# Attention and feed-forward on one core: where the maxima units of the next pair stand between the score tiles

## The chip, the cores and the metric

The kernel runs on 1 core of one Trainium2 chip. The metric is the device time of one execution in microseconds, as the median of several executions. The core has TensorE (PE: matmuls, and its weight loads, PEld), VectorE (DVE), ScalarE (ACT), GpSimd (POOL), and SyncE (SP), which issues most DMAs. Each has its own instruction stream, in order, and they wait for each other by semaphores. TensorE writes to PSUM, from where VectorE and ScalarE read.

## The reference

The inputs are q, k and v of 8 batches, 8 heads, 1152 positions and 64 features, and the weights w_in (512 x 2048) and w_out (2048 x 512).

```python
q_pool = q.reshape(B, H, S // factor, factor, D).mean(axis=3)          # 576 queries
scores = scale * np.matmul(q_pool, k.transpose(0, 1, 3, 2))            # 576 x 1152
scores = scores - np.max(scores, axis=-1, keepdims=True)
attn = np.exp(scores)
attn = attn / (np.sum(attn, axis=-1, keepdims=True) + 1e-09)
attn_out = np.matmul(attn, v)
x = attn_out.transpose(0, 2, 1, 3).reshape(B * S, H * D)               # 4608 x 512
h = x @ w_in
out = (h - np.tanh(h)) @ w_out
```

All of it is in fp32. Since the maximum of a query's scores is subtracted before the exponential, it has to be known (to some digits) before the scores of that query are used.

## The kernel before

There are two stages. The attention stage goes over 32 *pairs* (a pair is two heads of one batch; the two heads lie on the two halves of the 128 partitions). The feed-forward stage then goes over 9 chunks of 512 tokens. The change lies in the attention stage.

**A pair.** Its main loop (L475 to L491) has a score stage and a value stage of 18 *places* each. A place is one of 9 tiles of 128 keys for one of two halves of the queries, 288 of 576; so place 9 is key tile 0 of the second half, and a place of the score stage is called a tile below. At each place of the score stage `scores` (L278) issues eight matmuls of 288 columns into one PSUM tile: four terms, each for both heads. The terms are high part of the keys times high part of the queries (`kq_h` alone in the profile), high times low and low times high (`kq_l,kq_h` and `kq_h,kq_l`), and minus the maximum (`m_row,sel`). ScalarE then takes the exponential into a tile `p`, and POOL adds up three `p` tiles at a time (`add_p`, L295). In the value stage each place has two matmuls of `p` and `v` for each query half's output. Then `sums` adds the partial sums by matmuls with ones.

**The maxima.** The maxima of a pair are computed one pair ahead, by 14 *units*. A unit (`max_part`, L240) issues two matmuls of 384 columns, one for each head, from high parts alone, into one PSUM tile, and VectorE reduces it to maxima (`TENSOR_REDUCE mx<-ps 128x2`). Twelve units (0 to 11: four blocks of 128 queries by three thirds of the keys) are put behind places of the score stage of the pair before. Two more (12 and 13, for the last 64 queries of both heads, through `q_last`) stand behind the sums of the pair before that; unit 13 has one matmul and a narrow reduce (`128x1`). `max_row` (L258), at the last score place, turns the maxima into a row by a transpose and two DMAs through DRAM.

**The ring.** Score tiles, units, the two outputs of the value stage and the sums share one ring of four PSUM tiles of two banks each (L164), which are given out in turn in the order of the program. So each of them can be written only when the one four before it has been read: a score tile by ScalarE's exponential, a unit by VectorE's reduce.

**What sets the order.** Every engine's instructions stay in the order in which the program issues them (`InOrder`, L27). A table `at` lists functions to be called behind each place (`add`, L404; `run`, L470): the units (L407 to L413), the loads and splitting of later pairs (L414 to L425), and the first chunk of the feed-forward stage (L432 to L437), for which in the last pairs `x_r` is fetched from DRAM, and VectorE multiplies (place 8), ScalarE rounds (place 9) and VectorE subtracts (place 12). In the value stage four pieces of work on the weights go to VectorE and ScalarE.

Of the kernel before, what the change touches and what calls it, by code (L numbers as in the profile page):

```python
# [46 lines left out]
def attention_ffn_kernel(  # L47
# [107 lines left out]
    with ExitStack() as actx:  # L155
# [248 lines left out]
        def add(pi, place, f, *args):  # L404
            at.setdefault((pi, place), []).append(lambda: f(*args))

        for pi in range(1, n_pair):  # L407
            for i in range(12):
                add(pi - 1, i // 2 * 3 + 1 + i % 2, max_part, pi, i)
            if pi >= 2:  # L410
                for i in range(12, 14):
                    add(pi - 2, 2 * NS, max_part, pi, i)
            add(pi - 1, NS - 1, max_row, pi)  # L413
# [247 lines left out]
```

## Time and profile before

| | us |
|---|---|
| median of 3 runs | 1612.94 (1612.37 to 1613.27) |
| the profiled execution's own time | 1613.26 |
| its span, first to last instruction | 1611.5 |
| TensorE busy | 1578.1 (98%) |
| VectorE busy | 1207.5 (75%) |
| GpSimd busy | 1116.1 (69%) |
| ScalarE busy | 988.3 (61%) |
| mean granted TensorE clock | 0.996 |

All helpers issue through one line, L37, so the profile is read by engine and tile name: `ps<-kq_h` with 288 columns is a score matmul, with 384 columns one of a unit; `mx<-ps` is a unit's reduce, `p<-ps` an exponential. A row of a timeline has start, length, engine, line, operation, tiles, shape and count, and in brackets the idle time before it and what ended that. Alike instructions that follow each other are merged (x2, x4), from the first's start to the last's end. A TensorE instruction's length runs to its modelled end, so that matmuls overlap; what they occupy is the distance between starts. Where TensorE had to wait, the first matmul after the wait is listed from its weight load on, and the second one's start, less one matmul, gives the time from which it counts.

### The profile page before, as it was taken

What the parts mean: (1) busy time and instruction counts of PE and PEld (TensorE: products, weight loads), DVE (VectorE), ACT (ScalarE), POOL (GpSimd) and SP (SyncE); (2) the same over time, 40 slices, a digit from 0 to 9 for tenths busy, and PEclk for the clock granted to TensorE, in tenths of its full rate; (3) what the DMA queues carried; (4) which work ended last, traced back from release to release, by engine and by line L of the source; (5) the groups of instructions that cost most, each with busy time, mean ns of one, the idle gap of its engine ahead of it and who ended that gap; (6) DMA issues with size and microseconds to landing.
All of it is one profiled execution on the core that took longest, in us unless ns stands there. A gap on an engine that the chain in (4) does not pass through costs nothing.

```text
span 1611.5 us, 30812 instructions
## 1 busy us (share of the span) xinstructions
PE 1578.1 (98%) x12012; PEld 1224.9 (76%) x12012; DVE 1207.5 (75%) x1590; ACT 988.3 (61%) x1615; POOL 1116.1 (69%) x780
## 2 busy tenths in 40 slices
PE   5999999999999999998999999999999999999998
PEld 4777677777777777776678888888888888888886
DVE  6588788897878888766267777777777777777776
ACT  4676677676676677665455655565555555565554
POOL 3787787787787787786647566666657576666654
PEclk9999999999999999999999999999999999999999
DMA  5547767758577767637180201011010102020000
GB/s 174 170 145 209 224 197 228 215 173 281 160 241 209 232 195 222 178 115 221 62 329 14 66 13 66 7 42 38 7 66 14 66 14 66 13 67 14 27 1 27
DMA packets 84068, 193.59 MB, mean 120 GB/s; under 512 B 12370, under 2 KB 38994, under 8 KB 81874
## 3 DMA queue, kind: packets, MB, share of 16 engines
q1 hardware_dynamic: 79458, 164.20, 29.1%
q0 software_dynamic: 4464, 27.43, 8.7%
q8 instruction: 94, 1.54, 0.4%
q14 instruction: 52, 0.43, 0.1%
HBM read 126.12 MB, written 38.04 MB: 102 GB/s over the span
## 4 chain that ended last, share of the span: by engine, by line
PE 95%; DVE 2%; DMA 2%; ACT 1%; issue 0%; SPq 0%; POOLq 0%; POOL 0%; ACTq 0%; DVEq 0%
PE ps L37 46%; PE ps_h L37 25%; PE ps_o L37 24%; DMA x_r<-r_dram 1%; DVE mx L37 1%; DMA q<-in_q_dram 0%; DMA w_raw<-wi_dram 0%; DVE ps_w L37 0%; ACT g_s L37 0%; ACT kq_h L37 0%; ACT p L37 0%; DVE kq_l L37 0%; DVE x_r L37 0%; DMA m_dram<-tr 0%; SPq L37 0%
## 5 line engine op out<-in xcount | busy, mean ns | idle before, releaser
L37 DVE TENSOR_REDUCE mx<-ps 128x2 f32<-128x768 f32 x448 | 395.4, 924 | 117.3 <-PE ps L37 117.3
L37 ACT ACTIVATE p<-ps 128x576 f32<-128x576 f32 x576 | 353.1, 653 | 86.8 <-PE ps L37 62.7
L37 POOL TENSOR_TENSOR sum<-p,p 128x576 f32<-128x576 f32 x192 | 281.9, 1468 | 146.6 <-ACT p L37 146.6
L37 POOL TENSOR_SCALAR g_m<-g_u 128x512 uint8<-128x512 f32 (+1 forms) x145 | 246.9, 1703 | 195.7 <-ACT g_u L37 180.6
L37 POOL TENSOR_TENSOR sum<-sum,p 128x576 f32<-128x576 f32 x192 | 298.7, 1556 | 15.1
L37 PE MATMUL ps<-kq_h 64*128 64x288 f32 (+1 forms) x1920 | 286.1, 343 | 16.1 <-ACT kq_h L37 7.7
L37 PE MATMUL ps<-p,v 128*64 128x288 f32 x2304 | 286.4, 407 | 0.0
L37 POOL TENSOR_TENSOR g_lo<-g_s,g_hi 128x512 fp32r<-128x512 f32 (+1 forms) x145 | 186.6, 1287 | 93.7 <-ACT g_hi L37 93.7
L37 PEld LDWEIGHTS ps<-p,v 128*64 128x64 f32 x2304 | 162.6, 137 | 114.2 <-ACT p L37 6.6
L37 PE MATMUL ps_o<-w,g_hi 128*128 128x512 f32 x792 | 244.6, 390 | 1.0 <-ACT g_hi L37 1.0
L37 DVE SCALAR_TENSOR_TENSOR ps_w<-g_u,ps_h 128x512 f32<-128x512 f32 (+1 forms) x145 | 100.4, 692 | 187.6 <-ACT g_t L37 187.5
L37 ACT ACTIVATE g_u<-ps_h 128x512 f32<-128x512 f32 (+1 forms) x145 | 85.8, 592 | 241.9 <-PE ps_h L37 240.2
L37 PEld LDWEIGHTS ps<-kq_h 64*128 64x128 f32 x1920 | 181.9, 187 | 64.7 <-ACT p L37 27.5
L37 PE MATMUL ps_h<-x_h,w 128*128 128x512 f32 (+1 forms) x800 | 214.8, 390 | 0.0
L37 ACT ACTIVATE g_s<-g_u,pc 128x512 f32<-128x512 f32 x290 | 193.2, 714 | 11.9 <-ACT g_u L37 0.4
L37 PEld LDWEIGHTS ps_h<-x_h,w 128*128 128x128 f32 x800 | 149.7, 188 | 32.4
L37 PEld LDWEIGHTS ps_o<-w,g_hi 128*128 128x128 f32 x792 | 148.5, 188 | 33.6 <-ACT g_hi L37 1.4
L37 PE MATMUL ps<-kq_l,kq_h 64*128 64x288 f32 x1152 | 171.0, 293 | 0.0
L37 PE MATMUL ps<-kq_h,kq_l 64*128 64x288 f32 x1152 | 170.9, 293 | 0.0
L37 PE MATMUL ps<-m_row,sel 64*128 64x288 f32 x1152 | 170.8, 293 | 0.0
L37 PE MATMUL ps_o<-w,g_lo 128*128 128x512 f32 x396 | 154.8, 391 | 0.6 <-POOL g_lo L37 0.5
L37 DVE COPY_PREDICATED g_s<-g_m,g_t 128x512 f32<-128x512 uint8 (+1 forms) x145 | 111.0, 765 | 17.8 <-DVE g_t L37 3.7
(94 smaller groups left out, 2365.4 us busy)
## 6 DMA issues: line engine op xcount, KB each, us to landing
kq_l<-raw POOLq DMA_DIRECT2D x31, 864.0 KB, 10.7
raw<-in_k_dram SPq DMA_DIRECT2D x32, 576.0 KB
q<-in_q_dram SPq DMA_DIRECT2D x32, 576.0 KB
v<-in_v_dram SPq DMA_DIRECT2D x32, 576.0 KB
x_dram<-o_s SPq DMA_DIRECT2D x32, 288.0 KB
x_l<-x_dram SPq DMA_DIRECT2D x9, 1024.0 KB
out_dram<-o_f SPq DMA_DIRECT2D x36, 256.0 KB
w_raw<-in_w_in_dram SPq DMA_DIRECT2D x8, 1024.0 KB
```

The lines of the kernel that those rows point to most:

```text
L37: i = f(*args, **kwargs)
```

## The change

The twelve units of the next pair are called behind other places. Before, two stood behind each three key tiles: behind 1, 2, 4, 5, 7, 8, 10, 11, 13, 14, 16 and 17. Now they stand behind 0, 2, 3, 4, 5, 6, 8, 9, 11, 13, 15 and 17.

```diff
         for pi in range(1, n_pair):
             for i in range(12):
-                add(pi - 1, i // 2 * 3 + 1 + i % 2, max_part, pi, i)
+                add(pi - 1, (0, 2, 3, 4, 5, 6, 8, 9, 11, 13, 15, 17)[i], max_part, pi, i)
             if pi >= 2:
                 for i in range(12, 14):
                     add(pi - 2, 2 * NS, max_part, pi, i)
             add(pi - 1, NS - 1, max_row, pi)
```

On TensorE, the start of a pair (here pair 1; units 12 and 13 read `q_last`, `ps_594` is tile 0, 384 columns are a unit) stood so before, with the first matmul of each tile or unit and the engine that it waits for:

```order
L37 MATMUL ps_587<-kq_h_521,q_last0_122 128x384 [waits DVE_49,Activation_49]
...
L37 MATMUL ps_591<-kq_h_521,q_last0_122 128x384 [waits Activation_49]
L37 MATMUL ps_594<-kq_h_221 128x288 [waits Activation_49]
...
L37 MATMUL ps_605<-kq_h_221 128x288 [waits Activation_49]
...
L37 MATMUL ps_618<-kq_h_521 128x384 [waits DVE_49]
...
L37 MATMUL ps_622<-kq_h_221 128x288 [waits DVE_49]
...
L37 MATMUL ps_634<-kq_h_521 128x384 [waits Activation_49]
...
L37 MATMUL ps_640<-kq_h_221 128x288 [waits Activation_49]
```

and now:

```order
L37 MATMUL ps_594<-kq_h_221 128x288 [waits Activation_49]
...
L37 MATMUL ps_605<-kq_h_521 128x384 [waits Activation_49]
...
L37 MATMUL ps_609<-kq_h_221 128x288 [waits DVE_49]
...
L37 MATMUL ps_622<-kq_h_221 128x288 [waits DVE_49]
...
L37 MATMUL ps_634<-kq_h_521 128x384 [waits Activation_49]
...
L37 MATMUL ps_640<-kq_h_221 128x288 [waits DVE_49]
...
L37 MATMUL ps_651<-kq_h_521 128x384 [waits Activation_49]
...
L37 MATMUL ps_655<-kq_h_221 128x288 [waits Activation_49]
```

Unit 0 (`ps_605` now, `ps_618` before) has moved ahead of tile 1. Tile 1 (`ps_609`) has unit 12 four places before it and waits for VectorE, where tile 1 before (`ps_605`) had the sums and waited for ScalarE. Tile 3 (`ps_640`) now waits for unit 0's reduce.

On VectorE the units keep their order; only in the last pairs do they move past the operations on `x_r` and `x_l` of the first feed-forward chunk:

```order
-L37 TENSOR_REDUCE mx<-ps 128x2 x6
+L37 TENSOR_REDUCE mx<-ps 128x2 x7
 L37 TENSOR_TENSOR x_r<-x_l,x_r 128x512
 L37 TENSOR_REDUCE mx<-ps 128x2 x2
 L37 TENSOR_TENSOR x_l<-x_r,x_h 128x512
-L37 TENSOR_REDUCE mx<-ps 128x2 x4
+L37 TENSOR_REDUCE mx<-ps 128x2 x3
```

Seven of the twelve units, where there were six, stand ahead of the multiplication by `x_r`, and three, where there were four, behind the subtraction.

## The prediction

> **What bounds the kernel now.** I read the page first. TensorE fills the span, and nearly the whole chain of waits that ended last is its own.
>
> ```profile
> PE 1578.1 (98%) x12012; PEld 1224.9 (76%) x12012; DVE 1207.5 (75%) x1590; ACT 988.3 (61%) x1615; POOL 1116.1 (69%) x780
> PE 95%; DVE 2%; DMA 2%; ACT 1%; issue 0%; SPq 0%; POOLq 0%; POOL 0%; ACTq 0%; DVEq 0%
> ```
>
> That busy figure hides short waits, so I went to the stages: for one pair the score stage, the value stage, and the sums with the last two maxima units; then the score stage of the last pair but one, and of the last pair, which has no units in it.
>
> ```profile
> core 0: us, PE busy (x) PEld busy (x) DVE busy (x) ACT busy (x) POOL busy (x), PEclk, DMA share, GB/s
> 390.25:403.06 12.81, 12.81 (x169) 11.43 (x169) 11.00 (x13) 10.42 (x17) 10.42 (x8) 1.00 0.86 283
> 403.06:411.94 8.88, 8.88 (x74) 5.08 (x73) 7.54 (x9) 5.92 (x7) 8.72 (x6) 1.00 0.34 103
> 411.94:414.35 2.41, 2.41 (x31) 1.25 (x29) 1.61 (x4) 0.82 (x2) 0.21 (x1) 1.00 1.05 288
> 753.43:774.74 21.31, 15.40 (x168) 14.18 (x169) 13.23 (x15) 11.14 (x18) 14.54 (x11) 0.84 0.60 179
> 785.32:794.94 9.62, 9.62 (x144) 9.45 (x145) 0.00 (x0) 9.25 (x18) 7.33 (x6) 1.00 0.10 37
> ```
>
> A score stage without units takes 9.62 us; twelve units add 3.19, or 0.266 each. TensorE needs less for one. A score matmul of 288 columns follows the last after 0.13 us (the first four rows below), so a unit of 384 columns needs 0.13 x 384/288 = 0.175. Twelve are 2.1, so about 1.1 us of each score stage is waiting. The timelines of TensorE, its weight loads, VectorE and ScalarE show where, in the pair that starts at 414.25:
>
> ```profile
> 417.02 0.30 PE L37 MATMUL ps<-kq_h 64*128 64x288 f32 x2
> 417.15 0.30 PE L37 MATMUL ps<-kq_l,kq_h 64*128 64x288 f32 x2
> 417.28 0.30 PE L37 MATMUL ps<-kq_h,kq_l 64*128 64x288 f32 x2
> 417.41 0.30 PE L37 MATMUL ps<-m_row,sel 64*128 64x288 f32 x2
> ...
> 414.48 0.30 PE L37 MATMUL ps<-kq_l,kq_h 64*128 64x288 f32 x2
> 415.41 0.65 PE L37 MATMUL ps<-kq_h 64*128 64x384 f32 x4
> 415.89 0.29 PE L37 MATMUL ps<-kq_l,kq_h 64*128 64x288 f32 x2
> ...
> 426.90 0.34 PE L37 MATMUL ps<-kq_h 64*128 64x384 f32 x2
> 427.17 1.19 PE L37 MATMUL ps<-p,v 128*64 128x288 f32 x8
> ```
> ```profile
> 415.65 0.19 PEld L37 LDWEIGHTS ps<-kq_h 64*128 64x128 f32 x2 [0.19 <-DVE mx L37]
> 418.53 0.19 PEld L37 LDWEIGHTS ps<-kq_h 64*128 64x128 f32 x2 [0.15 <-ACT p L37]
> ```
> ```profile
> 414.18 1.42 DVE L37 TENSOR_REDUCE mx<-ps 128x2 f32<-128x768 f32 x2 [0.73 <-PE ps L37]
> 415.79 1.84 DVE L37 TENSOR_REDUCE mx<-ps 128x2 f32<-128x768 f32 x2 [0.19 <-PE ps L37]
> 417.93 1.82 DVE L37 TENSOR_REDUCE mx<-ps 128x2 f32<-128x768 f32 x2 [0.30 <-PE ps L37]
> 420.07 1.82 DVE L37 TENSOR_REDUCE mx<-ps 128x2 f32<-128x768 f32 x2 [0.33 <-PE ps L37]
> 415.15 1.19 ACT L37 ACTIVATE p<-ps 128x576 f32<-128x576 f32 x2 [1.07 <-PE ps L37]
> L37 DVE TENSOR_REDUCE mx<-ps 128x2 f32<-128x768 f32 x248 | 227.2, 953 | 61.3 <-PE ps L37 61.3
> L37 DVE TENSOR_REDUCE mx<-ps 128x1 f32<-128x384 f32 x19 | 10.4, 547 | 0.0
> L37 ACT ACTIVATE p<-ps 128x576 f32<-128x576 f32 x342 | 210.3, 650 | 50.6 <-PE ps L37 35.9 <-POOL sum L37 5.2
> ```
>
> A score tile or unit can be written only when the one four places ahead of it in the ring of four PSUM tiles has been read. Before the change three key tiles with two units repeat every 2.14 us (VectorE's rows at 417.93 and 420.07), against 3 x 0.53 + 2 x 0.175 = 1.94 of work. The 0.2 goes mostly on the tile behind the second unit, which waits for an exponential (idle 0.15 at 418.53). Neither ScalarE (two exponentials in 1.19, one 0.65: one each 0.54, 1.62 of 2.14) nor VectorE (idle 0.3 per three tiles) is full: it is the round trip through four tiles that binds.
>
> **The change part by part.** Nothing is added or removed: 31 x 12 units and their reduces keep their number, size and order among themselves, and the DMA queues of SP and POOL keep theirs. What moves is which tile stands four ahead. I cost the new order by the longest path through a pair, from five steps read off these rows (the trace has a third digit where the rows have two, and I use it). Time 0 is the first score matmul, 414.48 - 0.13 = 414.35.
> (a) A key tile is 0.53, a unit 0.175 on TensorE.
> (b) From a unit's matmul to its reduce: 415.41 to 415.79, 0.372.
> (c) A reduce lasts 0.954; two without idle time take 1.82 to 1.84, so the second starts 0.876 after the first.
> (d) From a reduce's end to TensorE at work again: 414.18 + 1.42 = 415.60 to 415.89 - 0.13 = 415.76, so 0.157.
> (e) From a tile's first matmul to its exponential 0.79, and 0.65 for that; from its end also 0.157.
>
> Run on the old order, these steps put the last unit at 12.54; the rows have 426.90 - 414.35 = 12.55. So the steps can be trusted to about 0.01 in an order that they know.
>
> New order. Unit 0 goes out at 0.53, directly behind tile 0. Tile 1 now has the wide unit 12 four places ahead, whose reduce ends at 414.18 + 0.954 = 415.13, or 0.79; so tile 1 starts at 0.95 where it could at 0.70: a wait of 0.24. (Before, the tile behind unit 0 waited 0.17 for the narrow unit's reduce, the row at 415.65.) Tile 2 follows at 1.48, the unit behind it at 2.01, its reduce at 2.38. From here VectorE has five units in a row, one behind each of tiles 2 to 6, and TensorE offers one every 0.7 us where a reduce takes 0.876: the reduces run without idle time, the fifth from 2.38 + 4 x 0.876 = 5.88 to 6.84. Tile 9 stands four places behind that unit, so it starts at 6.84 + 0.157 = 7.00. The unit behind it is reduced from 7.00 + 0.53 + 0.372 = 7.90 to 8.86; tile 12 waits for that until 9.02; two tiles on, the unit behind 13 goes out at 10.08 and is reduced by 11.41; tile 16 starts at 11.57, and the last unit at 12.63.
>
> So the sum for an ordinary pair is +0.09 (12.63 for 12.54). The rarer, shorter waits of tiles 10 to 17 (0.02 and 0.06 per two tiles) save about 0.4 us, and the first half gives more than that back: with seven units behind nine tiles VectorE sets its pace. The exponentials have slack all along this path.
>
> The value stage starts 0.27 behind the last unit in both orders (426.90 to 427.17), so the 0.09 passes on. The last reduce ends about 0.1 earlier against it, which helps VectorE's weight work and costs nothing. POOL starts its additions 0.4 later, since the second exponential moves from 1.34 to 1.7; its cover is this:
>
> ```profile
> 409.06 2.28 POOL L37 TENSOR_TENSOR sum<-sum,p 128x576 f32<-128x576 f32 x1
> 411.94 1.66 PE L37 MATMUL ps<-sum,ones 128*32 128x288 f32 x24
> ```
>
> Its last addition ends at 411.34, 0.6 ahead of the first sums matmul; 0.6 - 0.4 + 0.09 is left. Without that cover the price would be up to 0.3 a pair.
>
> The last pair but one is special: VectorE and, behind it, ScalarE wait for x_r from DRAM, and TensorE stands still until 767.92.
>
> ```profile
> 765.98 0.69 DVE L37 TENSOR_TENSOR x_r<-x_l,x_r 128x512 f32<-128x512 f32 x1 [5.00 <-DMA x_r<-r_dram]
> 766.58 1.81 DVE L37 TENSOR_REDUCE mx<-ps 128x2 f32<-128x768 f32 x2
> 767.24 1.17 ACT L37 ACTIVATE p<-ps 128x576 f32<-128x576 f32 x2
> 767.92 0.61 PE L37 MATMUL ps<-kq_h 64*128 64x288 f32 x2 [5.91 <-ACT p L37]
> 768.33 0.44 PE L37 MATMUL ps<-kq_l,kq_h 64*128 64x288 f32 x2
> 768.57 0.44 PE L37 MATMUL ps<-kq_h,kq_l 64*128 64x288 f32 x2
> ```
>
> The landing does not move. Tile 12 waited for an exponential that ended at 767.24 + 0.65; now it waits for the reduce that starts at 766.58 and ends at 767.54, 0.3 sooner. And one unit fewer is left: three instead of four, at the slow pace of 0.24 per matmul (768.33 to 768.57; the clock of that stage is 0.84) 0.32 each. Together -0.5, where a later landing would leave -0.3. In the pair before that, where VectorE has two more operations, the same steps give +0.08. The first pair I leave at 0: its first tiles run at the slow pace, where the reduces of units 12 and 13 are done in time.
>
> Sum: 29 x 0.09 - 0.5 = +2.1 us on the profiled execution's 1613.26 us, 1615.4. That execution lies 0.3 above the median of the runs, 1612.94, so the median should be 1615.0, 0.13% up.
>
> Bounds. A run of five reduces does not occur in the trace; runs of two do. At worst each would take its full 0.954: the path gains 4 x 0.08 = 0.31 and the old order loses a little too, +0.32 a pair. At best only the elements count: wide less narrow reduce is (953 - 547)/384 = 1.06 ns per element, 0.81 for 768, and other waits then bind: -0.03 a pair. I take 0.876, which is measured on this instruction back to back, and 0.86 to 0.89 as its doubt: +0.04 to +0.13 a pair.
> [...]
>
> **The rivals.**
> *Slower: the reduces of a run do not overlap.* Place: tiles 2 to 9 of each pair. From 0.90 per reduce on it costs 0.16 a pair or more; at 0.954, 29 x 0.32 - 0.5 = +8.8, 1621.7. For it: no run of five is on record, and POOL adds at the same time. Against: every run of two in the rows quoted takes 1.82 to 1.84 with POOL adding throughout. Chance 0.18.
> *Faster: VectorE comes to the pair earlier.* If unit 12's reduce ends before 0.54, tile 1 no longer waits, and with all of VectorE's work 0.4 sooner the path ends at 12.39: -0.15 a pair, 29 x -0.15 - 0.5 = -4.9, 1608.0. For it: VectorE idles 0.73 before that reduce (row at 414.18). Against: it idles for TensorE's own matmuls of unit 12, and nothing ahead of tile 0 moves. Chance 0.09.
> *No change: waits are traded one for one.* The old order loses 1.06 a pair in waits and the new 1.15 by my steps; an error of 0.02 in two or three steps makes them equal. Then only the -0.5 stays, and the few tenths of the first and last pairs: 1611.5 to 1614. Chance 0.20.
> The change does reach TensorE's queue as written, so that it does nothing at all is left out.
>
> **How the numbers follow.** The forecast has 0.53: 1615.0, alone 1614.0 to 1616.3. What a measurement of this kernel can tell from no change is 0.2%, 3.2 us, that is 1609.7 to 1616.2. Within it lie nearly all of the forecast and the traded waits, 0.69; above it, the non-overlapping reduces and the forecast's edge, 0.21; below it, most of the earlier VectorE and little else, 0.10. The range 1611.0 to 1618.5 takes in the forecast, the traded waits and the milder third of the slower case.
>
> **What would show it.** In the changed kernel's ordinary pairs the score stage should last 12.9 (12.81 now). Behind unit 0 a weight load should wait some 0.2 to 0.3 for a VectorE reduce. VectorE's row should merge five or more reduces in 4 x 0.876 + 0.954 = 4.46 us with no idle time, and the tile behind unit 8 should wait 0.17 for it. ScalarE's releases should no longer be the main ones in the weight loads' waits. The value stage should keep 8.88 and the sums 2.41. I am wrong if five reduces take over 4.6 us, if tile 1 starts by 0.75, or if a pair differs by more than 0.15.

## The result, and the profile after

The changed kernel takes 1616.49 us (median of 12 runs, 1612.64 to 1617.45) beside 1612.32 of the kernel before in the same comparison (12 runs, 1610.70 to 1614.11): a ratio of 1.0022, with 95% between 1.0013 and 1.0031. A second comparison on another occasion gave 1614.49 (11 runs) beside 1612.80 (27 runs), 1.0014 [1.0005, 1.0022]. So it is slower by 0.05 to 0.3%, on the edge of the 0.2% that can be told from no change; the forecast was 1615.0, 0.13% up.

The profiled execution took 1615.31 us, with a span of 1613.5 (1611.5 before). On the page, busy times and the chain's shares by engine are almost those of before; VectorE is busy for 11 us more (1218.6 for 1207.5) and has 3% of the chain instead of 2%:

```profile
PE 1580.7 (98%) x12012; PEld 1226.9 (76%) x12012; DVE 1218.6 (76%) x1590; ACT 991.1 (61%) x1615; POOL 1117.4 (69%) x780
PE 94%; DVE 3%; DMA 2%; ACT 1%; issue 0%; SPq 0%; POOLq 0%; POOL 0%; DVEq 0%; ACTq 0%
```

The stages of one pair (score, value, sums with the last two units), then the score stages of the last pair but one and of the last pair:

```profile
core 0: us, PE busy (x) PEld busy (x) DVE busy (x) ACT busy (x) POOL busy (x), PEclk, DMA share, GB/s
391.27:404.15 12.88, 12.88 (x168) 11.48 (x168) 11.24 (x13) 10.49 (x17) 10.10 (x8) 1.00 0.88 281
404.15:413.03 8.88, 8.88 (x74) 5.08 (x72) 7.42 (x8) 5.93 (x8) 8.72 (x6) 1.00 0.30 90
413.03:415.46 2.43, 2.43 (x31) 1.26 (x30) 1.95 (x4) 0.82 (x2) 0.55 (x1) 1.00 1.13 294
756.42:775.72 19.30, 14.54 (x168) 13.02 (x169) 13.34 (x15) 11.23 (x18) 13.37 (x10) 0.91 0.66 207
786.30:795.92 9.62, 9.62 (x144) 9.46 (x144) 0.00 (x0) 9.24 (x18) 7.32 (x6) 1.00 0.09 35
```

The score stage has grown from 12.81 to 12.88; value stage, sums and the stage without units are as they were (8.88, 2.43 here and 2.41 or 2.42 elsewhere, 9.62). The score stage of the last pair but one (the row at 756.42) is 2.0 shorter than before (21.31), which comes up below.

Inside the score stage, the pair that starts at 415.46. First VectorE's reduces, then two weight loads that waited, then TensorE, and last POOL's additions of the pair before and of this one around the sums' matmuls:

```profile
415.29 2.29 DVE L37 TENSOR_REDUCE mx<-ps 128x2 f32<-128x768 f32 x3 [0.41 <-PE ps L37]
417.84 4.42 DVE L37 TENSOR_REDUCE mx<-ps 128x2 f32<-128x768 f32 x5 [0.27 <-PE ps L37]
422.45 1.84 DVE L37 TENSOR_REDUCE mx<-ps 128x2 f32<-128x768 f32 x2 [0.20 <-PE ps L37]
...
416.29 0.19 PEld L37 LDWEIGHTS ps<-kq_h 64*128 64x128 f32 x2 [0.25 <-DVE mx L37]
422.31 0.19 PEld L37 LDWEIGHTS ps<-kq_h 64*128 64x128 f32 x2 [0.17 <-DVE mx L37]
...
415.59 0.29 PE L37 MATMUL ps<-kq_l,kq_h 64*128 64x288 f32 x2
...
416.54 0.29 PE L37 MATMUL ps<-kq_l,kq_h 64*128 64x288 f32 x2
...
422.54 0.29 PE L37 MATMUL ps<-kq_l,kq_h 64*128 64x288 f32 x2
...
428.08 0.34 PE L37 MATMUL ps<-kq_h 64*128 64x384 f32 x2
428.35 0.95 PE L37 MATMUL ps<-p,v 128*64 128x288 f32 x6
...
410.48 2.28 POOL L37 TENSOR_TENSOR sum<-sum,p 128x576 f32<-128x576 f32 x1
413.03 1.18 PE L37 MATMUL ps<-sum,ones 128*32 128x288 f32 x16
417.93 1.42 POOL L37 TENSOR_TENSOR sum<-p,p 128x576 f32<-128x576 f32 x1 [4.35 <-ACT p L37]
```

Five reduces run without idle time from 417.84 on, in 4.42. Two weight loads of the score stage wait for VectorE, by 0.25 (tile 1, behind unit 0) and by 0.17 (tile 9, behind the unit that follows tile 8, which the prediction calls unit 8). The value stage still starts 0.27 behind the last unit (428.08 to 428.35). POOL begins its additions 2.47 after the pair's start, where it was 2.07, and ended those of the pair before at 412.76, 0.27 ahead of the sums.

Over the pairs in the middle of the program the group of the score matmuls' weight loads shows who is waited for. Before:

```profile
L37 PEld LDWEIGHTS ps<-kq_h 64*128 64x128 f32 x1142 | 106.8, 183 | 27.4 <-ACT p L37 12.6 <-ACT s_s L37 4.9 <-DVE mx L37 3.6
```

and after, over the same pairs:

```profile
L37 PEld LDWEIGHTS ps<-kq_h 64*128 64x128 f32 x1142 | 106.7, 183 | 28.5 <-DVE mx L37 8.7 <-ACT s_s L37 5.0 <-ACT p L37 0.3
```

Among the waits that the row puts down to an engine, the exponentials (`p`) have fallen from 12.6 to 0.3, and the reduces (`mx`) have risen from 3.6 to 8.7. But the row names an engine only for waits of over 0.15 us, and the rest, 6.3 before and 14.5 after, is shorter ones. With those counted from the same traces, exponentials end 13.8 us of the waiting before and 8.6 after, reduces 8.7 and 14.9. So the reduces have become the main releaser, while the exponentials still hold TensorE up, for shorter times: in the pair shown, tiles 4 to 7 each start about 0.1 late, 0.16 behind the exponentials of tiles 2 to 5.

In the value stage VectorE's first large operation, the pooling of `q` for a later pair (`raw<-q`), has grown:

```profile
L37 DVE TENSOR_TENSOR raw<-q 128x576 f32<-128x576 f32 x32 | 35.0, 1094 | 4.7 <-DMA q<-in_q_dram 4.7
```

is the group before, and after it is

```profile
L37 DVE TENSOR_TENSOR raw<-q 128x576 f32<-128x576 f32 x32 | 46.5, 1453 | 4.6 <-DMA q<-in_q_dram 4.6
```

In an ordinary pair it lasts 1.54 where it lasted 1.10, and that accounts for VectorE's 11 us. It starts 0.11 earlier against the value stage and ends 0.33 later. It now runs beside POOL's first addition of the value stage for 0.9 us, before for 0.5; whether that is the cause, no run here shows.

**Where the 2.0 us of the span went.** From the starts of the pairs in the two traces:

| stretch | before | after | difference |
|---|---|---|---|
| start to pair 0 | 27.41 | 27.26 | -0.15 |
| pair 0 | 24.80 | 25.08 | +0.28 |
| an ordinary pair, start to start | 24.105 | 24.189 | +0.084 |
| pairs 1 to 28, summed | 675.49 | 678.24 | +2.75 |
| pair 29 | 25.73 | 25.84 | +0.11 |
| pair 30 | 31.89 | 29.88 | -2.01 |
| pair 31 to the first product with w_out | 34.30 | 35.28 | +0.98 |
| the rest | 791.86 | 791.93 | +0.07 |

Of the +2.75, 28 x 0.084 = 2.35 is the ordinary pair; the other 0.4 comes from single pairs that are longer than their neighbours (4 and 7 before; 9, 21 and 26 after, 0.2 to 0.35 each). These belong to the order and not to the execution, since every other profile of the same orders has the same pairs (4 and 7 with the early fetch too; 9, 21 and 26 in the second profile of the changed kernel and with the early fetch). For 9 and 21 the trace after shows the cause. Here is the start of pair 9, at 245.79:

```profile
244.83 1.21 DVE L37 SCALAR_TENSOR_TENSOR w_hl<-w_raw,w_t 128x1024 int32<-128x1024 int32 x1
245.96 2.28 DVE L37 TENSOR_REDUCE mx<-ps 128x2 f32<-128x768 f32 x3
...
246.96 0.19 PEld L37 LDWEIGHTS ps<-kq_h 64*128 64x128 f32 x2 [0.59 <-DVE mx L37]
```

VectorE's work on the weights, 0.33 later for the longer operation on `q`, still runs when unit 12 is ready, so its reduce starts 0.17 behind the pair's start where it otherwise starts 0.17 ahead of it, and tile 1 waits 0.59 instead of 0.25. In the kernel before, the same piece of work ends in time for that reduce. What lengthens pairs 4, 7 and 26 is not shown. The two large terms of opposite sign sit behind two standstills of TensorE, 5.91 us before and 4.76 after in pair 30, 3.43 and 3.44 in the feed-forward part. In pair 30 it waits for x_r:

```profile
768.66 0.69 DVE L37 TENSOR_TENSOR x_r<-x_l,x_r 128x512 f32<-128x512 f32 x1 [4.29 <-DMA x_r<-r_dram]
770.27 0.40 PE L37 MATMUL ps<-kq_h 64*128 64x288 f32 x2 [4.76 <-DVE mx L37]
770.92 0.45 PE L37 MATMUL ps<-m_row,sel 64*128 64x288 f32 x2
771.16 0.45 PE L37 MATMUL ps<-kq_h 64*128 64x288 f32 x2
```

VectorE's multiplication behind the landing came 12.24 after the pair's start, 12.55 before (765.98 less 753.43). Behind it the matmuls follow each other by 0.24 again, at a granted clock of 0.91 in this stage and 0.84 before. In the feed-forward part the second group of matmuls for h (`ps_h`) starts 3.4 us behind the last matmul in both kernels. Before:

```profile
815.31 2.08 PE L37 MATMUL ps_h<-x_h,w_hl 128*128 128x512 f32 x4 [3.43 <-DVE g_t L37]
817.18 1.66 PE L37 MATMUL ps_h<-x_l,w_hl 128*128 128x512 f32 x4
818.68 1.09 PE L37 MATMUL ps_h<-x_h,w_hl 128*128 128x512 f32 x4
```

and after:

```profile
816.29 2.07 PE L37 MATMUL ps_h<-x_h,w_hl 128*128 128x512 f32 x4 [3.44 <-DVE g_t L37]
818.17 1.91 PE L37 MATMUL ps_h<-x_l,w_hl 128*128 128x512 f32 x4
819.87 1.91 PE L37 MATMUL ps_h<-x_h,w_hl 128*128 128x512 f32 x4
```

Four matmuls take 1.09 at a granted clock of 1.00 and 1.91 at 0.50; here the slow stretch lasted longer after than before. That is a matter of the execution, not of the change: over the profiles of all kernels with this feed-forward part the stretch from pair 31 to w_out takes either 34.1 to 34.5 or 35.3, and a second profile of the changed kernel had 34.07. Pair 30 takes 29.9 to 34.3 in the profiles that fetch x_r where the kernel before does.

In the kernel before, the granted clock is 0.50 from 767.22 to 774.05 and from 815.01 to 818.42; in the changed one, from 770.59 to 774.00 and from 814.96 to 821.79. In the other stretches between 30 and 1600 us it is 1.00. So a slow stretch begins within 1.4 us of the end of each of the two standstills, and lasts 6.83 and 3.41 us before, 3.41 and 6.83 after. In the one in pair 30 a score matmul follows the last after 0.24, in an ordinary pair after 0.13. What starts and ends a slow stretch, and why its length differs, no run here shows.

### The profile page after: what moved, and what is told of

It is laid out like the page before. It is cut to its first block, busy times and chain, and to the rows that moved or that the text cites. A ratio compares the mean times of both kernels' runs of the same rounds, so it can differ in the third digit from the quotient of the medians.

```text
span 1613.5 us, 30812 instructions
## 1 busy us (share of the span) xinstructions
PE 1580.7 (98%) x12012; PEld 1226.9 (76%) x12012; DVE 1218.6 (76%) x1590; ACT 991.1 (61%) x1615; POOL 1117.4 (69%) x780
## 3 DMA queue, kind: packets, MB, share of 16 engines
q8 instruction: 94, 1.54, 0.4%
## 4 chain that ended last, share of the span: by engine, by line
PE 94%; DVE 3%; DMA 2%; ACT 1%; issue 0%; SPq 0%; POOLq 0%; POOL 0%; DVEq 0%; ACTq 0%
PE ps L37 45%; PE ps_h L37 25%; PE ps_o L37 24%; DVE mx L37 1%; DMA x_r<-r_dram 1%; ACT kq_h L37 0%; DVE w_t L37 0%; DMA q<-in_q_dram 0%; DVE raw L37 0%; DMA w_raw<-wi_dram 0%; DVE w_hl L37 0%; DVE ps_w L37 0%; ACT g_s L37 0%; ACT w_t L37 0%; DVE kq_l L37 0%
```

## The experiments

In the whole study the score stage of one ordinary pair (the others differ by up to 0.03) and the period, the median distance from pair to pair, come from the profile, the time and its ratio to the kernel before (with 95%) from the runs:

| kernel | score stage | period | time, us | ratio |
|---|---|---|---|---|
| before | 12.81 | 24.105 | 1612.8 to 1613.4 | 1 |
| the change again | 12.88 | 24.18 | 1614.49 | 1.0014 [1.0005, 1.0022] |
| unit 0 back behind tile 1 | 12.82 | 24.125 | 1615.12 | 1.0010 [1.0001, 1.0019] |
| first half new, second old | 12.96 | 24.267 | 1619.47 | 1.0042 [1.0028, 1.0055] |
| first half old, second new | 12.75 | 24.049 | 1613.12 | 1.0002 [0.9992, 1.0011] |
| before, half reduces | 12.75 | 24.067 | 1606.97 | 0.9968 [0.9957, 0.9978] |
| changed, half reduces | 12.57 | 23.887 | 1599.99 | 0.9925 [0.9910, 0.9940] |
| spread order | 12.65 | 23.961 | 1610.34 | 0.9988 [0.9979, 0.9997] |
| spread, early fetch | 12.65 | 23.956 | 1604.89 | 0.9954 [0.9942, 0.9967] |
| before, early fetch | 12.82 | 24.105 | 1606.85 | 0.9962 [0.9948, 0.9975] |
| changed, early fetch | 12.90 | 24.187 | 1609.26 | 0.9976 [0.9968, 0.9985] |
| two orders, early fetch | 12.66 | 23.954 | 1602.17 | 0.9932 [0.9919, 0.9944] |
| changed, units 12 and 13 exchanged | 12.65 | 23.958 | 1610.47 | 0.9983 [0.9974, 0.9992] |

**The change once more**, unedited, for the size of the scatter.

> The changed order once more, unchanged, for a second profile. Theory (the path through VectorE's run of reduces, +0.08 us in each of 29 ordinary pairs, some jitter at the two places where TensorE restarts from a standstill): score stage 12.88 in ordinary pairs again, 1614 to 1617; the stage of the last pair but one and the first two feed-forward steps differ from profile to profile by up to 2 us. Rival (the last pairs lose something of their own in the changed order): the last pair but one or the pair before it is longer than in the old order by 1 us or more in this profile too.

Measured: the score stage again 12.88, pair 30 at 30.52 and the feed-forward stretch at 34.07, where the first profile had 29.88 and 35.28. Each run also records its mean granted clock, and the time goes with it: of these eleven, two at 0.999 took 1612.5 and 1612.7, four at 0.998 took 1614.1 to 1614.5, one at 0.997 took 1614.9 and four at 0.996 took 1615.8 to 1616.8. In the first comparison nine of twelve were at 0.996 (1616.3 to 1617.5). So the two medians, +4.2 and +1.7, go with how often the granted clock was low; that the stretches behind the two standstills are where it was low (0.50) is read from the profiled executions alone.

**One unit moved back**: unit 0 behind tile 1 again.

```diff
-                add(pi - 1, (0, 2, 3, 4, 5, 6, 8, 9, 11, 13, 15, 17)[i], max_part, pi, i)
+                add(pi - 1, (1, 2, 3, 4, 5, 6, 8, 9, 11, 13, 15, 17)[i], max_part, pi, i)
```

> One place changed back: unit 0 stands behind tile 1, as before the change; the run behind tiles 2 to 6 stays. Theory (tile 1's wait for unit 12's reduce starts VectorE's run late, and the run carries it to the end): score stage 12.79, 0.09 less than in the changed order; time 1612 to 1613, that of the old order. Rival (five reduces in a row cost by themselves): 12.88, 1614.5 to 1616.5.

Measured: 12.82, by 0.03 more than the steps gave, and most of the change's cost is gone from the pair (period 24.125). VectorE's run is now six reduces long, since unit 0 has joined it, but starts 1.43 behind the pair's start. That agrees with a path that begins at tile 1's wait for unit 12's reduce; the exchange of units 12 and 13 below shows it. The whole time, 1615.12, lies where the rival put it and can't be told from that of the changed kernel. In the profile pair 29 took 26.75 where it takes 25.84 with the change, and the feed-forward stretch was the long one, 35.3. The score stage of pair 29 was 15.45:

```profile
728.27:743.72 15.45, 13.20 (x169) 11.48 (x169) 14.36 (x15) 10.87 (x18) 13.05 (x9) 1.00 0.59 170
```

The steps for ordinary pairs do not cover this one, where VectorE also works on `x_r` and `x_l` and the order of the units decides which of them stand behind that; VectorE is busy for 14.36 of the 15.45, TensorE for 13.20.

**Each half alone.**

```diff
-                add(pi - 1, (0, 2, 3, 4, 5, 6, 8, 9, 11, 13, 15, 17)[i], max_part, pi, i)
+                add(pi - 1, (0, 2, 3, 4, 5, 6, 8, 10, 11, 13, 16, 17)[i], max_part, pi, i)
```

> The first half of the changed order alone (0, 2, 3, 4, 5, 6, 8), with five units of the old pattern behind it (10, 11, 13, 16, 17). Theory: the first half loses, and the changed order's second half gives part of it back; here nothing is given back: score stage 12.96, 0.16 above the old order's, time 1616.5 to 1618.5. Rival (the loss is tile 1's wait alone, 0.24 in place of 0.17, and the second half is neutral): 12.88, 1614.5 to 1616.5.

```diff
-                add(pi - 1, (0, 2, 3, 4, 5, 6, 8, 9, 11, 13, 15, 17)[i], max_part, pi, i)
+                add(pi - 1, (1, 2, 4, 5, 7, 8, 9, 11, 13, 15, 16, 17)[i], max_part, pi, i)
```

> The old first half (1, 2, 4, 5, 7, 8) with the spacing of the changed order's second half (9, 11, 13, 15, 16, 17). Theory: 12.76, 0.04 below the old order, since exponentials are waited for less; time 1610.5 to 1612. Rival (second half neutral): 12.80, 1612 to 1613.

Measured: 12.96 and 12.75, each within 0.01 of its expectation. The dense first half loses 0.15 to 0.16 of a pair; the thinner second half gives 0.06 to 0.08 back, whichever first half stands before it. Both times came out about 1 us above what was expected. The first kernel's profile has a long pair 30 (34.28); the second's has 0.9 more in pair 0 (25.67), 0.7 more in pair 30 (32.58) and 0.4 more in single longer pairs than the kernel before.

**The reduces cut in two.** Both orders with `tensor_reduce` over half of each unit's columns. Half of the keys are left out of the maxima, so these kernels compute another thing, and their times serve the comparison alone.

```diff
-                dve.tensor_reduce(w.mx[:, t, c], ps[:, :, 0:CH], axis=AX.X, op=ALU.max)
+                dve.tensor_reduce(w.mx[:, t, c], ps[:, :, 0:CH // 2], axis=AX.X, op=ALU.max)
```

With the order of before:

> The old order with the twelve reduces cut to half of each head's columns (0:CH // 2), so that the maxima of half of the keys are left out and a reduce should take about 0.55 us, as the narrow one does. Theory (the old order loses its time to exponentials four tiles back, not to reduces): score stage 12.76 instead of 12.81; time 1611 to 1612.5. Rival (VectorE sets the pace of both orders): 12.4 or less, 1600 to 1606.

With the changed order:

> The changed order with the same twelve reduces cut to half of their columns (half of the keys left out of the maxima). Theory (its path runs through the reduces): score stage 12.56 instead of 12.88, now below the old order; time 1604 to 1608. Rival (the loss is TensorE's own, from switching between score tiles and units more often): stays at 12.8 or above, 1612 to 1616.

Measured in the old order,

```profile
409.24:421.99 12.75, 12.75 (x168) 11.44 (x168) 7.38 (x13) 10.43 (x18) 10.37 (x8) 1.00 0.75 199
```

and in the changed order:

```profile
406.58:419.15 12.57, 12.57 (x169) 11.47 (x169) 7.29 (x13) 10.41 (x17) 9.86 (x7) 1.00 0.63 174
408.95 1.26 DVE L37 TENSOR_REDUCE mx<-ps 128x2 f32<-128x384 f32 x2 [0.66 <-PE ps L37]
414.00 0.19 PEld L37 LDWEIGHTS ps<-kq_h 64*128 64x128 f32 x2 [0.21 <-ACT p L37]
```

With the reduces halved, the period of before falls by 0.04 and the changed one by 0.30, and their order turns round: the changed kernel is then 0.18 a pair faster. Its run of five is gone (VectorE idles between the reduces), and behind tile 1 the longest waits of the weight loads are for exponentials (0.21 in the row above). So the length of the reduces is what made the new order slower, and not TensorE's more frequent change between tiles and units, which is the same here. The times came out 4 us below what was expected, both of them, and the cause is at the other end: pair 0's own units are reduced one after another before its first score, which came at 22.3 and 22.5 here instead of 27.4 and 27.3. The kernel of before, in its start-up:

```profile
8.41 7.87 DVE L37 TENSOR_REDUCE mx<-ps 128x2 f32<-128x768 f32 x9 [1.50 <-PE ps L37]
```

and with half reduces:

```profile
8.07 4.27 DVE L37 TENSOR_REDUCE mx<-ps 128x2 f32<-128x384 f32 x9 [1.50 <-PE ps L37]
```

**An order without the run.** The steps of the prediction, applied to other tables, give a shorter path when the units are spread with no more than three reduces in a row.

```diff
-                add(pi - 1, (0, 2, 3, 4, 5, 6, 8, 9, 11, 13, 15, 17)[i], max_part, pi, i)
+                add(pi - 1, (1, 2, 4, 5, 6, 8, 9, 11, 12, 13, 16, 17)[i], max_part, pi, i)
```

> Units behind tiles 1, 2, 4, 5, 6, 8, 9, 11, 12, 13, 16 and 17: an order picked by the five steps of the prediction so that no run on VectorE is longer than three and few tiles stand four behind an exponential that is just out. Theory: score stage 12.62, 0.19 below the old order; time 1606 to 1608.5. Rival (the steps hold for the orders they were read from, and a new order finds another wait): 12.75 or above, 1611 and up.

Measured: 12.65 for 12.62, a gain of 0.15 on the old order that the steps foresaw to 0.03. The time fell less than expected, to 1610.34: in the profile pair 29 took 0.7 more than before (26.44), the single longer pairs 0.6 more (1.1 in sum), and the feed-forward stretch was the long one (35.3).

**The standstill in pair 30 taken away.** The fourth fetch of x_r is issued behind place 14 of pair 29's score stage instead of in its value stage, so that x_r is there when VectorE wants it.

```diff
-            add(h_x + c // 2, (11, NS + 14)[c % 2], lambda c=c: x0[0].fetch_r(c))
+            add(h_x + c // 2, (11, NS + 14 if c < 3 else 14)[c % 2], lambda c=c: x0[0].fetch_r(c))
```

With the spread order:

> The same order, and the fourth x_r of the first feed-forward chunk fetched behind place 14 of the score stage of pair 29 instead of place 14 of its value stage, about 11 us sooner. Theory: its landing no longer stops VectorE in pair 30, whose score stage falls from 20 to 22 us to 14.5 and keeps the full clock; time 1598 to 1602. Rival (the transfer lands no sooner, since the weights' loads hold the same queues): score stage of pair 30 still over 18, time within 2 us of the order alone.

With the order of before:

> The old order with the earlier fetch of the fourth x_r alone, so that the standstill in pair 30, which jitters by up to 2 us, is out of the comparison with the next run. Theory: pair 30 falls to 25 to 26 us; time 1606.5 to 1608, 5 to 6 below the kernel before. Rival (the earlier fetch only paid in the spread order): above 1610.

With the changed order:

> The changed order with the same earlier fetch. Theory (the change costs 0.08 us in each of 30 pairs and nothing else): 2.3 to 2.8 us above the old order with the fetch, 1609 to 1610.5. Rival (the last pairs carry a cost of their own, as the medians' 3.6 us might say): 3.5 us or more above it.

In the old order VectorE now multiplies by x_r without a wait, and pair 30's score stage falls from 21.31 to 14.46:

```profile
761.31 0.99 DVE L37 TENSOR_TENSOR x_r<-x_l,x_r 128x512 f32<-128x512 f32 x1
753.86:768.32 14.46, 13.29 (x168) 11.44 (x168) 13.46 (x15) 11.06 (x18) 12.07 (x8) 1.00 0.82 255
```

In the changed order it is 14.54:

```profile
756.97:771.51 14.54, 13.30 (x168) 11.52 (x168) 13.43 (x15) 11.01 (x18) 11.74 (x8) 1.00 0.80 254
```

With that scatter gone, the runs stand clear of each other: 1606.81 to 1607.06 for the old order (5 runs), 1608.66 to 1610.23 for the changed one (11 runs). The medians differ by 2.4 us, 0.15%, as expected, and that is the cost of the change by itself. It is near 29 x 0.084 = 2.4, but no closer than the runs of the changed kernel scatter (1.6): in the two profiles pairs 1 to 28 alone differ by 2.74, longer single pairs included. The spread order with the early fetch fell short of what was expected (1604.89 for 1598 to 1602). The fetch gave 5.5 of it; the order alone had already come out 2 us above its own expectation, and pairs 29 and 30 both take 15.15 for a score stage, 1.4 more in sum than in the old order.

**Two orders in one kernel**: the spread order, the early fetch, and for the units called in the last two pairs that have any an order that leaves VectorE room for x_r.

```diff
-                add(pi - 1, (0, 2, 3, 4, 5, 6, 8, 9, 11, 13, 15, 17)[i], max_part, pi, i)
+                add(pi - 1, ((1, 2, 3, 4, 5, 6, 9, 10, 14, 15, 16, 17) if pi > n_pair - 3 else (1, 2, 4, 5, 6, 8, 9, 11, 12, 13, 16, 17))[i], max_part, pi, i)
```

> The spread order and the earlier fetch, and in pairs 29 and 30, where VectorE also works on x_r and x_l, the order 1, 2, 3, 4, 5, 6, 9, 10, 14, 15, 16, 17, which keeps units off VectorE while that work stands there. Theory: score stages of these two pairs 13.1 instead of 15.15 each; time 1600 to 1602. Rival (other waits in these pairs): above 14.5, 1604 and up.

```profile
724.66:738.59 13.93, 13.37 (x169) 11.58 (x169) 13.39 (x15) 11.03 (x19) 11.54 (x8) 1.00 0.72 204
749.90:763.82 13.92, 13.41 (x168) 11.67 (x169) 13.73 (x15) 11.21 (x19) 11.54 (x8) 1.00 0.97 324
```

Those two score stages fall to 13.9, from 15.15 (13.1 was expected), and the time, 1602.17, is 0.2 above the range expected. At 1602.17 it is the fastest kernel of the study that computes the reference, 0.68% under the kernel before.

**The run kept, its start moved.** The changed order with units 12 and 13 called in the other order, so that the narrow unit 13 stands four places ahead of tile 1 and is reduced first, and the wide unit 12 stands behind it.

```diff
-                for i in range(12, 14):
+                for i in (13, 12):
```

> The changed order with units 12 and 13 exchanged behind the sums, so that tile 1 has the narrow reduce four places ahead. Theory (the path starts with unit 12's reduce, through tile 1): tile 1 no longer waits for VectorE and starts at 0.70, VectorE's run starts about 0.15 sooner, and the score stage takes 12.70 to 12.80 instead of 12.88; time 1611 to 1613.5. Rival (the run's pace alone decides, wherever it starts): 12.88 again, 1614 to 1616.5.

```profile
412.64:425.29 12.65, 12.65 (x168) 11.51 (x168) 11.06 (x13) 10.43 (x17) 10.10 (x8) 1.00 0.77 206
414.79 4.42 DVE L37 TENSOR_REDUCE mx<-ps 128x2 f32<-128x768 f32 x5 [0.20 <-PE ps L37]
419.26 0.19 PEld L37 LDWEIGHTS ps<-kq_h 64*128 64x128 f32 x2 [0.17 <-DVE mx L37]
```

The run still lasts 4.42 and tile 9 still waits 0.17 for it, but the run starts 2.15 after the pair's start instead of 2.38, and the score stage is 0.23 shorter, 0.05 better than the lower end of what was expected; the time, 1610.47, is 0.5 below its range. Nothing else of the change was touched, and the pair is now 0.15 shorter than before (23.958 for 24.105). The whole time is 0.17% below that of before, still within the 0.2%. A run of five is thus not dear by itself. So the change's cost is the sum of two things in a row on one path: a late start, set by unit 12's reduce, and a run that goes at VectorE's pace from there.

## Why the prediction was right or wrong

**The term for an ordinary pair was right**: +0.09 predicted, +0.084 measured in the period, 12.88 for a score stage expected at 12.9. The two medians, 1616.49 and 1614.49, lie on both sides of 1615.0, the first 0.2 beyond the forecast's own upper end. The steps, one by one:

- Tile 1 waits for unit 12's reduce: 0.24 foretold, 0.25 at the weight load; tile 1 counts from 0.95 in both (416.54 - 0.13 - 415.46). The two kernels that remove this wait (unit 0 moved back, units 12 and 13 exchanged) lose most of the cost, or all of it.
- The run of five: begins at 417.84 - 415.46 = 2.38 as foretold, and takes 4.42, not 4.46. The pace is (4.42 - 0.954)/4 = 0.867, where 0.876 was taken. So tile 9 starts at 422.54 - 0.13 - 415.46 = 6.95 instead of 7.00; 0.01 of that is left at the last unit.
- Tile 9 waits 0.17 for the fifth reduce, as foretold. The last unit, foretold at 12.63, comes at 428.08 - 415.46 = 12.62.
- "The exponentials have slack all along this path" did not hold for TensorE, and it did no harm. In the run, four places are two tiles and two units, so by the prediction's own steps (d) and (e) a tile can follow the one two tiles ahead of it only after 0.79 + 0.65 + 0.157 = 1.60. Tiles 4 to 7 do wait about 0.1 each for the exponentials of tiles 2 to 5, and TensorE offers VectorE a unit every 0.80 us and not every 0.7. A reduce takes 0.867 from start to start, and so VectorE still set the pace, but by 0.06 a unit where 0.17 was counted on.
- "The last reduce ends about 0.1 earlier against it, which helps VectorE's weight work and costs nothing" was wrong. It does end 0.12 earlier, but the operation on `q` behind it became longer by 0.44, the weight work came 0.33 later, and in pairs 9 and 21 tile 1 paid for it. The sum had no term for these, 0.7 us together.
- The value stage and the sums kept their length, and POOL started 0.4 later with 0.27 of its cover left, where 0.29 was worked out.

**The rival "the reduces of a run do not overlap" is refuted** by the row of 4.42; five times 0.954 would be 4.77, over the mark of 4.6 that was set. And the chance of 0.18 for it was too high for a plain reason: the prediction says that a run of five does not occur in the trace of before, but a run of nine does, in the start-up (the row at 8.41 quoted above). (7.87 - 0.954)/8 = 0.865 was there to be read. What that row alone could not tell is the pace with POOL adding at the same time, since POOL is idle there (busy 0.00 of the 7.87).

**The rival "VectorE comes earlier" did not come true** as an effect of this order: VectorE still idles 0.41 for unit 12's matmuls. That an earlier reduce of the right unit is worth 0.2 a pair is shown by the exchange of units 12 and 13.

**"Waits are traded one for one" was close.** Waits were traded, from the exponentials to the reduces, but not evenly: 0.084 a pair stays.

**What was mis-sized lies outside the ordinary pairs, and the total was right partly by luck.** The term for pair 30 was -0.5; it measured -2.0 in one profile and -1.4 in the other. The 0.5 was worked out with the landing of x_r held still and the clock's slow stretch too. Between the two traces the multiplication behind the landing moved from 12.55 to 12.24 after the pair's start, and the slow stretch from 6.83 to 3.41 us; two executions of the changed kernel differ by 0.64 in this pair (29.88 and 30.52). No term stood for the feed-forward's restart either, +0.98 in one profile and -0.23 in the other. Pair 0, taken as 0, measured +0.28 and +0.06; over the kernels with this start it scatters between 24.7 and 25.8, so that is not told apart from nothing. The sum of +2.1 agreed with the +2.0 of the profiled execution because errors cancelled: pair 30 gave 1.5 more than was put down, and against it stood the restart's +1.0, pair 0's +0.3 and the longer single pairs' +0.4. With pair 30's standstill taken out of both kernels the change costs +2.4.

That the first comparison stands at +4.2, twice the forecast, and the second at +1.7 goes with the granted clock of the runs. Whether the changed order makes the long slow stretches more frequent, or whether twelve runs fell that way, no run settles.

## What to carry to other kernels

In a ring of shared buffers, work the longest path through the whole order, from five durations read off the trace: that foretold the ordinary score stage of every kernel here to 0.04 of 12.8 us, but for the exchange of units 12 and 13, which did better by 0.05 than the best that was expected. Ask of each tile which one stands a ring's length ahead of it and when that one is read; an order that fills the consumer's queue early makes a run, and the run's start matters as much as its pace. A profile row that names releasers for long waits alone can make one look gone that has only become short, so look at the tiles' own starts too. And the places where such an order meets other work (the last pairs, with x_r on VectorE) need a path of their own: there the orders of this study differ by up to 1.5 us in one pair (26.75 and 25.24 for pair 29).

## What the runs showed that had not been expected

- The start-up is bound by VectorE: halving the reduces brought the first score from 27.4 to 22.3 us, more than all pairs together gained from any order of the study with full reduces.
- Behind the two standstills the slow clock (0.50) costs a varying time: it lasted 3.41 or 6.83 us in the two traces, and the same feed-forward stretch took either 34.1 to 34.5 or 35.3 us. With the standstill of pair 30 removed, the kernel before needs 1606.85 us and its 5 runs lie within 0.25 us, where 21 runs lay within 3.4; the changed kernel's 11 runs still scatter by 1.6.
- A single fetch issued half a pair earlier was worth 6 us to the kernel before (0.9962), far more than the change under study moved.
